# A one-core attention and two-layer MoE kernel: one unit's logits moved, a one-block order rewritten, filler products recounted

## The chip, the cores and the metric

The kernel runs on one core of a Trainium2 chip. The metric is device time in microseconds (us) of one execution; lower is better. In the profile PE is TensorE's matmuls, PEld its weight loads, DVE is VectorE, ACT is ScalarE, POOL is GpSimd and SP is SyncE; a q behind an engine's name is its sequencer or its DMA issue.

## The reference

A linear-attention recurrence over 768 steps (2 batches, 8 heads of 48) gives x with 1536 tokens of 384 numbers. Two mixture-of-experts layers follow, each with 8 experts (384 to 1024 to 384). The first adds a bias per modality to the logits; the second has a capacity of 384 tokens per expert:

```python
logits = x @ w_gate + modality_bias[modality_id]     # layer 0
e_idx = np.argmax(logits, axis=1); gate_w = softmax(logits)[e_idx]
out[mask] = gate_w[mask, None] * (np.maximum(x[mask] @ w1[e], 0.0) @ w2[e])
# layer 1: the same on layer 0's output, without a bias, tokens past the capacity give 0
```

So layer 1's routing needs the logits of layer 0's output, for all tokens.

## The kernel before

Three parts run one after the other: attention (L186 to L602), MoE layer 0 and MoE layer 1, both by `moe()` (L954).

**Units.** A layer's tokens are gathered by expert into blocks of 128; up to two blocks of one expert are a unit. Six units (0 to 5) always run, up to 13 may. On these data layer 0 runs eight (0 to 7) and layer 1 ten. `body(j)` (L1277) reads the unit's kind from the routing and branches to `two(j)` (L1221, both blocks, weights stationary) or `one(j)` (L1165, block 1 alone, tokens stationary). In layer 0 units 6 and 7 are one-block units (branch at L1295, where `one` comes first), the rest two-block; in layer 1 units 1, 2, 7 and 8 are one-block (branch at L1300).

**Precision.** Every fp32 product is three products of high and low parts. The high parts of the next unit's weights are made by ACT (`hi`, L960), the low parts by DVE (`lo`, L963): ten pieces per unit, six of w1 (letters a to f, 512 wide) and four of w2 (g to j, 768 wide).

**The order is written by hand** (a manual schedule on all engines): each engine's queue is the program's order. In `one`, six stretches of side work stand between the main steps first(j,0), first(j,1), turn(j,0), turn(j,1), second(j,0), second(j,1); each takes one string of `ONE` (L75). Its letters: a to j a weight piece for the next unit (capital: the low part alone); 0 and 1 the relu of a half (`relu`, L1057: ACT at L1063, DVE at L1065); y and z the turn and the split of the previous unit's block 1 (`yturn3` L1137, `ysplit3` L1145); l its logits (`ylog3` L1149); x and X the turn of the next unit's block 0 or 1 (`xprep` L1015: three PE transposes, an ACT copy L1020, a DVE subtraction L1021); P and Q the gates (Q is a DVE reduce L1034 and a reciprocal L1035). `turn` (L1068) transposes the relu's result on PE (L1072), ACT copies it (hh, L1075), DVE subtracts (hl, L1076), and `second` (L1079, products at L1088) consumes both.

**Layer 1's logits in layer 0's tail.** `ylog3` computes a block's logits with nine bf16 products (L722), a DVE reduce (L723) and then the block's store (`store`, L1132, an indirect DMA issued by POOL). Units 0 to 4 do block 0's in the next unit; unit 5 does it within its own last products (`end`, L1270 to L1273), since it could be the last unit.

**The end of layer 0.** `rest(j)` (L1361) branches on the number of blocks (L1372): the next unit, or `last(j-1)` (L1324). `last` loads the logits of all stored tokens back from memory (lgd, SP, L1337), scales the last block (ACT L1343), transposes it (PE L1347), copies (ACT L1348), takes its logits (`logits`, PE L696), spreads them by a one-hot product (DVE L1350, PE L1351) and adds both (DVE L1354). `routing()` (L758) follows. Ahead of them in the program stand unit forms that this input doesn't take.

**Filler.** `warm()` (L752) runs products of ones while PE would wait: `WARM[i] * 512 / width` products, width from `WIDE` (L46). Indices 0 to 2 are in the routing, 3 and 4 ahead of a layer's first unit, around `xprep(0,1)` and before the transposes of L1317.

Of the kernel before, what the change touches and what calls it, by code (L numbers as in the profile page):

```python
# [9 lines left out]
F32 = mybir.dt.float32  # L10
# [18 lines left out]
P = 128  # L29
NC = N // P  # L30
KD = DM // P
KF = F // P
U = 2 * P
NU_MIN = N // U
# [8 lines left out]


WARM = (4, 12, 2, 15, 4)
WIDE = ((512, 512, 512, 512, 512), (512, 512, 128, 128, 128))  # L46
TP = (3, 4)
OHP = ((0, 6), (6, 10), (10, 12))
CEIL = 255.0 / 512.0
# [20 lines left out]
SCALE = 'ssv'  # L70
LATE = (1,)
ONE_FIRST = (6, 7)
RELU = "sv"
PB = (1, 3, 1, 2)
ONE = (('ecadfPyz', '01bQ', 'X', 'l', 'hgix', 'js'), ('badec0P', 'f1hQ', 'xX', 'i', 'j', 'g'))  # L75


class Ctx:
# [875 lines left out]
def moe(tc, c, m, route, run, layer, src, w1d, w2d, dst, wg2, wp2, zb, following, lgs=None, psum=None, bad=None, general=None, ykeep=None):  # L954
    nc = tc.nc
    n = f"_m{layer}{run}"
# [5 lines left out]
    def lo(p, eng):  # L962
        eng.tensor_sub(p[2], p[0], p[1].bitcast(F32))  # L963
# [12 lines left out]
    with ctx:  # L976
        ap = m.ap
        if psum is None:
            psum = ctx.enter_context(tc.tile_pool(name="mo_ps" + n, bufs=2, space=PSUM))
# [32 lines left out]
                hi(pc[i], nc.scalar)  # L1012
                lo(pc[i], nc.vector)

        def xprep(j, t):  # L1015
            ts = slice(t * P, t * P + P)
            pt = psum.tile([P, KD, P], F32, tag="tp", name=f"xp{j}{t}" + n, bufs=TP[layer])
            for kc in range(KD):
                nc.tensor.transpose(pt[:, kc], m.xg[j % 2][:, t, kc * P : (kc + 1) * P], c.ident)  # L1019
            nc.scalar.copy(m.xh[j % 2][:, :, ts], pt)  # L1020
            nc.vector.tensor_sub(m.xl[j % 2][:, :, ts], pt, m.xh[j % 2][:, :, ts].bitcast(F32))  # L1021
# [35 lines left out]
        def relu(j, half):  # L1057
            ph = st.pop(("p", j, half))
            h = ap.tile([P, 512], F32, tag=f"h{half}", name=f"h{j}{half}" + n, bufs=1)
            wd = 512 if half == 0 or j == 0 else 256  # L1060
            for a in range(0, 512, wd):
                if RELU[half] == "s" or wd == 512:
                    nc.scalar.activation(h[:, a : a + wd], ph[:, a : a + wd], AF.Relu)  # L1063
                else:
                    nc.vector.tensor_scalar(h[:, a : a + wd], ph[:, a : a + wd], 0.0, None, ALU.max)  # L1065
            st["h", j, half] = h
# [82 lines left out]
        def ylog3(j, t):  # L1149
            logits3(tc, psum, [m.yp], wp2, m.yo[j % 2][:, t : t + 1, DM:XW], f"_y{j}{t}" + n, "lg", 1)  # L1150
            store(j, t)
# [13 lines left out]
        def one(j, pc):  # L1165
            before = layer == 0 and j > 0
            plan = iter(ONE[layer])

            def work():
                for p in next(plan):  # L1170
                    if p == "x" or p == "X":
                        if j + 1 < NU:
                            xprep(j + 1, int(p == "X"))
                    elif p == "y":
                        if before:
                            if j < NU_MIN:
                                ylog3(j - 1, 0)
                            yturn3(j - 1, 1)
                    elif p == "z":
                        if before:  # L1180
                            ysplit3()
                    elif p == "l":
                        if before:
                            ylog3(j - 1, 1)
                    elif p == "P" or p == "Q":
                        gates(j, 1 + (p == "Q"))
                    elif p == "s":
                        if layer == 0 and j < NU_MIN - 1:
                            scale(j, 1, "s")
                    elif p == "0" or p == "1":  # L1190
                        relu(j, int(p))
                    else:
                        i = "abcdefghij".index(p.lower())
                        if pc:
                            if p.islower():
                                hi(pc[i], nc.scalar)
                            lo(pc[i], nc.vector)

            first(j, 0)
            own(j, 0)  # L1200
            work()
            first(j, 1)
            own(j, 1)
            work()
            turn(j, 0)
            work()
            turn(j, 1)
            own(j, 2)
            work()
            second(j, 0)  # L1210
            work()
            second(j, 1)
            work()
# [7 lines left out]
        def two(j, pc):  # L1221
            before = layer == 0 and j > 0
            first2(j, 0)
            if before:
                if j < NU_MIN:
                    ylog3(j - 1, 0)
                yturn3(j - 1, 1)
                ysplit3()
            gates(j, 1)
            own(j, 0)  # L1230
            if j or layer:
                split(pc, 0, 2)
            first2(j, 1)
            gates(j, 2)
            own(j, 1)
            if j or layer:
                split(pc, 2, 6)
            else:
                split(pc, 0, 3)
            second2(j, 0, 0)  # L1240
            if before:
                ylog3(j - 1, 1)
            first2(j, 2)
            own(j, 2)
            if j or layer:
                split(pc, 6, 9)
            else:
                split(pc, 3, 6)
            second2(j, 0, 1)
            first2(j, 3)  # L1250
            if j == layer == 0:
                split(pc, 6, 8)
            else:
                split(pc, 9, 10)
            second2(j, 1, 0)
            second2(j, 2, 0)
            if j + 1 < NU:
                for t in range(2):
                    xprep(j + 1, t)
            second2(j, 3, 0)  # L1260
            scale(j, 0, SCALE[1])
            if j == layer == 0:
                split(pc, 8, 10)

            def turned():
                yturn3(j, 0)
                ysplit3()


            end = layer == 0 and j >= NU_MIN - 1  # L1270
            second2(j, 1, 1, (turned, 4) if end else None)
            second2(j, 2, 1, (turned, 2) if layer == 0 and not end else None)
            second2(j, 3, 1, (lambda: ylog3(j, 0), 4) if end else None)  # L1273
            if layer == 0 and not end:
                scale(j, 1, "s")

        def body(j):  # L1277
# [46 lines left out]
        def last(j):  # L1324
            if layer:
                finish(j)
            else:

                sp = ap.tile([P, 512], F32, tag="h0", name=f"sp{j}" + n, bufs=1)
                ohp, ohc = sp[:, 0:P], sp[:, P : P + NC]  # L1330
                put = sp[:, P + NC : P + NC * (E + 1)].rearrange("p (c e) -> p c e", e=E)
                col = slice(2 * j + 1, 2 * j + 2)
                nc.vector.tensor_scalar(ohp, c.i1[:, :, 0], R.tp[:, col], None, ALU.is_equal)
                nc.vector.tensor_scalar(ohc, c.jx[:, 0:NC], R.tc[:, col], None, ALU.is_equal)

                pl = psum.tile([P, NC, E], F32, tag="tp", name=f"lq{j}" + n, bufs=TP[0])
                nc.sync.dma_start(lgs[0], dst.rearrange("(p j) e -> p j e", j=NC)[:, :, DM:XW])  # L1337
                er = EXPERT0[j % 2]
                m.raw.load(j % 2, *following, slice(er, er + 1), parts=(1,))

                for kc in range(KD):
                    ks = slice(kc * P, kc * P + P)
                    nc.scalar.activation(m.yo[j % 2][:, 1, ks], ykeep[1][:, ks], AF.Identity, scale=R.gate[:, col])  # L1343
                xT = ap.tile([P, KD, P], F32, tag="lxT", name=f"lx{j}" + n, bufs=1)
                for kc in range(KD):
                    pt = psum.tile([P, P], F32, tag="h" if kc == 1 else "tp", name=f"yt{j}{kc}" + n, bufs=2 if kc == 1 else TP[0])
                    nc.tensor.transpose(pt, m.yo[j % 2][:, 1, kc * P : (kc + 1) * P], c.ident)  # L1347
                    nc.scalar.copy(xT[:, kc], pt)  # L1348
                py = logits(tc, psum, [xT[:, kc] for kc in range(KD)], wg2, None, None, f"_y{j}1" + n, "lg", 1)
                nc.vector.tensor_tensor(put, py.unsqueeze(1).to_broadcast((P, NC, E)), ohc.unsqueeze(2).to_broadcast((P, NC, E)), ALU.mult)  # L1350
                nc.tensor.matmul(pl, lhsT=ohp, rhs=put, start=True, stop=True)  # L1351
                nc.vector.tensor_copy(m.yo[j % 2][:, 1, DM:XW], py)
                store(j, 1)
                nc.vector.tensor_add(lgs[1], lgs[0], pl)  # L1354

                if j % 2 == 0:
                    for p in p0:
                        hi(p, nc.scalar)
                        lo(p, nc.vector)
# [142 lines left out]
```

## Time and profile before

| | us |
|---|---|
| median of 3 runs | 452.92 (452.83 to 454.48) |
| profiled execution, its own time | 451.07 |
| its span | 449.3 |
| mean granted TensorE clock | 0.979 of full speed |

Busy shares of the span: PE 93%, PEld 85%, DVE 73%, ACT 55%, POOL 32%. By the timeline, unit 5 of layer 0 runs from 220.9 to about 241, unit 6 to 252.3, unit 7 to 264.9; `last(7)` runs from 267.2 to 273.5, layer 1's routing to 282.6, and layer 1's first real products start at 287.5. A line of a timeline gives start and duration in us, engine, source line, operation, output<-inputs, shapes, a count, and in brackets the engine's idle time before it with what ended it.

### The profile page before, as it was taken

How to read it: one execution, taken by the hardware profiler on the slowest of the kernel's cores; microseconds unless marked ns; L12 is line 12 of the kernel's file. 1: busy time of each engine (PE TensorE's matmuls, PEld its weight loads, DVE VectorE, ACT ScalarE, POOL GpSimd, SP SyncE). 2: the span in 40 equal slices, each digit the busy share in tenths (PEclk: the TensorE clock that was granted, in tenths of full speed). 3: DMA queues.
4: the chain of work that ended last, by engine and by line, in shares of the span. 5: the costliest groups of instructions: out<-in, count | busy, mean ns of one | idle time of the engine just before them, and what ended most of it. 6: DMA issues, size and time to landing. Idle time of an engine off the chain costs nothing. (4 is left out here: it accounts for less than half of the span.)

```text
span 449.3 us, 9663 instructions
## 1 busy us (share of the span) xinstructions
PE 417.9 (93%) x3270; PEld 380.1 (85%) x3275; DVE 329.5 (73%) x677; ACT 249.3 (55%) x508; POOL 143.3 (32%) x160
## 2 busy tenths in 40 slices
PE   8999999999899999999999956999999999999990
PEld 4789988987389999999997854899899999998990
DVE  7798867984879859677597975386974945859760
ACT  3256545543537647557475840277864755777650
POOL 5637963141230422213223300503343132124420
PEclk9999999999899999999999996999999999999996
DMA  6987237348630121366744945314887657761100
GB/s 113 200 148 152 48 56 194 74 169 324 197 91 2 56 79 54 109 205 222 256 147 134 292 129 154 91 20 131 319 281 258 228 187 232 237 230 52 50 22 20
DMA packets 85590, 66.98 MB, mean 149 GB/s; under 512 B 60586, under 2 KB 77655, under 8 KB 85504
## 3 DMA queue, kind: packets, MB, share of 16 engines
q1 hardware_dynamic: 80512, 52.30, 39.8%
q0 software_dynamic: 4992, 13.61, 9.9%
q8 instruction: 44, 0.72, 0.7%
q14 instruction: 42, 0.34, 0.2%
HBM read 95.63 MB, written 11.56 MB: 239 GB/s over the span
## 5 line engine op out<-in xcount | busy, mean ns | idle before, releaser
L963 DVE TENSOR_TENSOR w1l<-w1r,w1h 128x512 fp32r<-128x512 f32 x114 | 71.7, 686 | 9.6 <-ACT w1h L960 9.4
L963 DVE TENSOR_TENSOR w2l<-w2r,w2h 128x768 fp32r<-128x768 f32 x76 | 69.2, 951 | 0.3 <-ACT w2h L960 0.3
L960 ACT CAST w1h<-w1r 128x512 fp32r<-128x512 f32 x114 | 62.7, 617 | 0.3 <-DMA xs<-zv 0.3
L1107 DVE SCALAR_TENSOR_TENSOR qhl_m<-qh_m,qhh_m 128x512 fp32r<-128x512 f32 x48 | 33.0, 686 | 36.0 <-ACT qhh_m L1106 36.0
L960 ACT CAST w2h<-w2r 128x768 fp32r<-128x768 f32 x76 | 59.4, 835 | 0.0
L1106 ACT ACTIVATE qhh_m<-qh_m 128x512 fp32r<-128x512 f32 x48 | 28.8, 599 | 41.7 <-PE qh_m L1101 41.7
L1101 PE MATMUL qh_m<-xh,w1h 128*128 128x256 f32 x288 | 51.0, 286 | 0.3 <-ACT xh L1318 0.2
L1101 PE MATMUL qh_m<-xl,w1h 128*128 128x256 f32 x288 | 50.2, 283 | 0.6 <-DVE w2l L963 0.6
L1119 PE MATMUL y_m<-w2h,qhh_m 128*128 128x384 f32 x192 | 50.0, 341 | 0.0
L1101 PE MATMUL qh_m<-xh,w1l 128*128 128x256 f32 x288 | 49.8, 282 | 0.0
L1119 PE MATMUL y_m<-w2l,qhh_m 128*128 128x384 f32 x192 | 49.6, 339 | 0.0
L1119 PE MATMUL y_m<-w2h,qhl_m 128*128 128x384 f32 x192 | 49.3, 338 | 0.0
L1004 POOL DMA_INDIRECT xg<-x,idg_l x24 | 26.0, 1083 | 69.2 <-DVE gd L1029 43.3
L1004 POOL DMA_INDIRECT xg<-xs,idg_l x20 | 22.2, 1111 | 67.2 <-issue 54.7
L1101 PEld LDWEIGHTS qh_m<-xh,w1h 128*128 128x128 f32 x288 | 42.6, 188 | 0.8 <-ACT xh L1318 0.8
L1101 PEld LDWEIGHTS qh_m<-xl,w1h 128*128 128x128 f32 x288 | 40.9, 188 | 1.2 <-DVE w2l L963 1.0
L1101 PEld LDWEIGHTS qh_m<-xh,w1l 128*128 128x128 f32 x288 | 40.9, 188 | 0.0
L1132 POOL DMA_INDIRECT out_dram<-yo,ids_l x20 | 22.1, 1103 | 49.3 <-ACT w2h L960 11.5
L1127 ACT ACTIVATE yo<-y_m,gate_l 128x384 f32<-128x384 f32 x29 | 16.9, 582 | 36.6 <-PE y_m L1119 28.9
L1020 ACT CAST xh<-xp_m 128x384 fp32r<-128x384 f32 x38 | 16.7, 485 | 35.8 <-PE xp_m L1019 35.8
L397 ACT ACTIVATE X<-endt,Sb 112x112 f32<-112x112 f32 x40 | 14.2, 354 | 38.5 <-PE endt L387 27.2
L1132 POOL DMA_INDIRECT x<-yo,ids_l x14 | 17.5, 1251 | 54.4 <-DVE qhl_m L1107 23.9
(252 smaller groups left out, 892.9 us busy)
## 6 DMA issues: line engine op xcount, KB each, us to landing
w2r<-in_moe_w_dram SPq DMA_DIRECT2D x50, 768.0 KB
w1r<-in_moe_w_dram SPq DMA_DIRECT2D x72, 512.0 KB
xs<-zv SPq DMA_DIRECT2D x12, 192.0 KB
out_dram<-zt SPq DMA_DIRECT2D x4, 576.0 KB
raw_w<-in_w_dram SPq DMA_DIRECT2D x14, 144.0 KB
raw_r<-in_r_dram SPq DMA_DIRECT2D x14, 144.0 KB
raw_k<-in_k_dram SPq DMA_DIRECT2D x14, 144.0 KB
raw_v<-in_v_dram SPq DMA_DIRECT2D x14, 144.0 KB
```

Source lines behind the costliest of these rows:

```text
L397: nc.scalar.activation(Xn, z, AF.Identity, scale=Tn)
L960: (eng.copy if eng is nc.scalar else eng.tensor_copy)(p[1], p[0])
L963: eng.tensor_sub(p[2], p[0], p[1].bitcast(F32))
L1004: nc.gpsimd.indirect_dma_start(out=m.xg[j % 2][:, t], out_offset=None, in_=src, in_offset=bass.IndirectOffsetOnAxis(ap=R.idg[:, 2 * j + t ...
L1020: nc.scalar.copy(m.xh[j % 2][:, :, ts], pt)
L1101: nc.tensor.matmul(ph[:, f], lhsT=w[s][:, kc, fs], rhs=a[s][:, kc], start=(i == 0), stop=(i == 3 * KD - 1))
L1106: nc.scalar.activation(hh, ph, AF.Relu)
L1107: nc.vector.scalar_tensor_tensor(hl, ph, 0.0, hh.bitcast(F32), ALU.max, ALU.subtract)
L1119: nc.tensor.matmul(st["y", j, t], lhsT=a[:, f, ts], rhs=w[s][:, 2 * q + f], start=(q == 0 and i == 0), stop=(q == 3 and i == 5))
L1127: nc.scalar.activation(m.yo[j % 2][:, t, 0:DM], py, AF.Identity, scale=R.gate[:, 2 * j + t : 2 * j + t + 1])
L1132: nc.gpsimd.indirect_dma_start(out=dst, out_offset=bass.IndirectOffsetOnAxis(ap=R.ids[:, 2 * j + t : 2 * j + t + 1], axis=0), in_=m.yo[j % ...
```

## The change

Five edits:

- `WIDE`: layer 1's filler 2 and 3 (8 and 60 products of 128 columns) become 2 and 15 products of 512 columns.
- `RELU`: in layer 0's one-block form the second half's relu goes from DVE to ACT, still as two pieces of 256.
- `ONE[0]`: z moves behind the relu of half 0, Q from the second stretch to the fifth, x from the fifth to the fourth (ahead of second(j,0)).
- x in layer 0's one-block form takes a PSUM buffer of tag "h" in place of "tp".
- Block 0's logits and store of unit 5 leave unit 5's tail: they are in unit 6, or in `last(5)` where there is no unit 6. Unit 5's `yturn3`/`ysplit3` of block 0 moves from within second2(5,1,1) to within second2(5,2,1).

```diff
-WIDE = ((512, 512, 512, 512, 512), (512, 512, 128, 128, 128))
+WIDE = ((512, 512, 512, 512, 512), (512, 512, 512, 512, 128))
-RELU = "sv"
+RELU = ("ss", "sv")
-ONE = (('ecadfPyz', '01bQ', 'X', 'l', 'hgix', 'js'), ('badec0P', 'f1hQ', 'xX', 'i', 'j', 'g'))
+ONE = (('ecadfPy', '01zb', 'X', 'lx', 'Qhgi', 'js'), ('badec0P', 'f1hQ', 'xX', 'i', 'j', 'g'))
-        def xprep(j, t):
+        def xprep(j, t, tag="tp"):
-            pt = psum.tile([P, KD, P], F32, tag="tp", name=f"xp{j}{t}" + n, bufs=TP[layer])
+            pt = psum.tile([P, KD, P], F32, tag=tag, name=f"xp{j}{t}" + n, bufs=TP[layer] if tag == "tp" else 2)
-                if RELU[half] == "s" or wd == 512:
+                if RELU[layer][half] == "s" or wd == 512:
-                            xprep(j + 1, int(p == "X"))
+                            xprep(j + 1, int(p == "X"), "h" if p == "x" and layer == 0 else "tp")
...
-                            if j < NU_MIN:
+                            if j <= NU_MIN:
                                 ylog3(j - 1, 0)
...
-            end = layer == 0 and j >= NU_MIN - 1
+            end = layer == 0 and j >= NU_MIN
             second2(j, 1, 1, (turned, 4) if end else None)
             second2(j, 2, 1, (turned, 2) if layer == 0 and not end else None)
             second2(j, 3, 1, (lambda: ylog3(j, 0), 4) if end else None)
-            if layer == 0 and not end:
+            if layer == 0 and j < NU_MIN - 1:
                 scale(j, 1, "s")
...
+                if j < NU_MIN:
+                    ylog3(j, 0)
                 pl = psum.tile([P, NC, E], F32, tag="tp", name=f"lq{j}" + n, bufs=TP[0])
```

The `j <= NU_MIN` line stands in `one` and in `two`; the last two lines added are in `last`.

## Rows read from the trace of the kernel before

**Rows 1.** Stretches: length; PE, PEld, DVE, ACT, POOL busy (count); clock, DMA share, GB/s
```profile
241.30:252.30 11.00, 10.96 (x78) 10.21 (x79) 10.42 (x22) 9.08 (x17) 4.36 (x4) 1.00 0.88 268
252.30:265.00 12.70, 11.04 (x78) 9.87 (x77) 12.15 (x26) 9.56 (x18) 3.75 (x3) 1.00 0.75 250
265.00:273.30 8.30, 2.65 (x11) 2.22 (x11) 2.01 (x7) 1.52 (x6) 0.00 (x0) 0.79 0.40 86
273.30:287.50 14.20, 11.66 (x120) 8.16 (x122) 8.53 (x37) 0.83 (x4) 5.06 (x5) 0.88 0.39 126
```

**Rows 2.** Timeline, the end of unit 5 and the start of unit 6
```profile
239.66 0.52 PE L722 MATMUL l_y_m<-wp,yp 128*128 128x24 bf16 x9
...
241.34 0.48 PE L1053 MATMUL ph_m<-w1h,xh 128*128 128x512 f32 x1 [0.72 <-ACT yo L1127]
...
241.84 0.69 DVE L963 TENSOR_TENSOR w1l<-w1r,w1h 128x512 fp32r<-128x512 f32 x1 [0.48 <-ACT w1h L960]
```

**Rows 3.** Timeline of DVE, PE and ACT, the middle of unit 7
```profile
258.85 0.75 DVE L1065 TENSOR_SCALAR h_m<-ph_m 128x256 f32<-128x256 f32 x2
...
259.32 0.77 PE L1072 MATMUL hp_m<-ident,h_m 128*128 128x128 f32 x4 [1.56 <-DVE h_m L1065]
...
259.52 0.68 DVE L963 TENSOR_TENSOR w1l<-w1r,w1h 128x512 fp32r<-128x512 f32 x1
...
260.12 0.17 DVE L1034 TENSOR_REDUCE gm<-gd 128x2 f32<-128x18 f32 x1
...
260.13 0.59 ACT L1075 CAST hh_m<-hp_m 128x512 fp32r<-128x512 f32 x1 [1.69 <-PE hp_m L1072]
...
260.40 0.67 DVE L1076 TENSOR_TENSOR hl_m<-hp_m,hh_m 128x512 fp32r<-128x512 f32 x1
...
261.45 0.68 DVE L1076 TENSOR_TENSOR hl_m<-hp_m,hh_m 128x512 fp32r<-128x512 f32 x1
...
262.05 0.17 DVE L723 TENSOR_REDUCE yo<-l_y_m 128x8 f32<-128x24 f32 x1
```

**Rows 4.** Groups by line and form: busy us, mean ns of one, idle before
```profile
L1020 ACT CAST xh<-xp_m 128x384 fp32r<-128x384 f32 x38 | 16.7, 485 | 35.8 <-PE xp_m L1019 35.8
...
L1065 DVE TENSOR_SCALAR h_m<-ph_m 128x256 f32<-128x256 f32 x12 | 4.5, 416 | 0.0
L1063 ACT ACTIVATE h_m<-ph_m 128x512 f32<-128x512 f32 x6 | 3.6, 599 | 0.1
```

**Rows 5.** Line 1372, 262 to 270 us: durations min/median/max in ns, first and last start
```profile
L1372 PEldq COMPARE_BRANCH  x1: 4701/4701/4701, 262.9 to 262.9; - x1
```

**Rows 6.** Timeline from unit 7's end to the last logits of layer 0
```profile
263.00 1.02 POOL L1132 DMA_INDIRECT x<-yo,ids_l  x1 [5.24 <-ACT w2h L960]
...
267.69 0.60 SPq L1337 DMA_DIRECT2D lgd<-x  x1
...
270.92 1.24 PE L696 MATMUL lpl_y_m<-wg,lx_m 128*128 128x8 f32 x6 [2.49 <-issue]
...
273.28 0.26 DVE L1354 TENSOR_TENSOR lg<-lgd,lq_m 128x96 f32<-128x96 f32 x1 [0.76 <-PE lq_m L1351]
```

**Rows 7.** Line 1132, 262 to 275 us: POOL's waits, and its transfers' landing
```profile
L1132 POOLq EVENT_SEMAPHORE  x4: 17/834/5985, 256.3 to 270.9; - x4
...
DMA to landing us min/median/max: 4.7/4.8/4.9
```

**Rows 8.** DMA view, 17.5 to 82 us: instruction packets, MB, share
```profile
q8 instruction: 6, 0.10, 0.6%
```

**Rows 9.** Stretch of straight code in the attention, columns as in rows 1
```profile
17.50:82.00 64.50, 62.84 (x639) 55.47 (x639) 51.62 (x82) 34.34 (x92) 38.26 (x50) 1.00 0.65 130
```

**Rows 10.** Timeline, PE ahead of layer 1's first unit
```profile
281.34 3.51 PE L755 MATMUL warm_m<-i,ones 128*128 128x128 bf16 x60
...
286.78 0.55 PE L1317 MATMUL xp_m<-ident,xg 128*128 128x128 f32 x3 [0.70 <-DMA xg<-x,idg_l]
```

**Rows 11.** Line 1300, layer 1, 288 to 440 us: PE's branches into a unit's form
```profile
L1300 PEldq COMPARE_BRANCH  x15: 65/191/419, 302.2 to 434.3; - x15
```

More of the change, by code (lines that the diff above doesn't have):

```diff
@@ L1224, in two @@
             if before:
-                if j < NU_MIN:
+                if j <= NU_MIN:
                     ylog3(j - 1, 0)
```

## The prediction

> **What bounds the kernel now.** The page first: PE is busy 93% of the span, so over the kernel as a whole only TensorE counts, and an edit that takes work from DVE or ACT should be worth nothing. The stretches view corrects this for the place where nearly all of the change lies [rows 1]. In units 6 and 7 DVE is busy 10.42 of 11.00 and 12.15 of 12.70 us: there DVE is the full engine. PE waits for it: before unit 7's second turn it sits idle 1.56 us until DVE's relu is done [rows 3]. In the next stretch, `last(7)`, nobody is busy: PE works 2.65 of 8.30 us. That stretch is pure waiting, and the timeline shows on what. PE's branch at L1372, out of unit 7 over the forms not taken, lasts 4.70 us [rows 5]; after it, PE stops once more for 2.49 us between two products of one group (L696), and the releaser given is "issue": it waited for no data [rows 6].
>
> That branch starts at 262.9. The last thing that PE's queue waits for ahead of it is hl of unit 7's second half, DVE's subtraction at 261.45 + 0.68 = 262.13 [rows 3]. So the tail of layer 0 is timed by DVE's chain through units 6 and 7, then by a jump, then by that stop. All my sums are for the end of L1354, which begins at 273.28 [rows 6]; the routing follows it directly.
>
> **Unit 5's tail.** The logits of block 0 sit in PE's queue ahead of the last two products, and they wait for DVE's split. PE then reads unit 6's branch after that wait, and sits idle 0.72 us before unit 6's first product; DVE's first low part follows at 241.84 after 0.48 us of waiting for ACT's high part [rows 2]. Without the logits' wait, the branch is read while earlier products still run. PE gains up to 0.37 us (the logits' slot, 239.66 to 240.03 by the count of products that follow) and most of the 0.72. DVE, which matters, gains between 0 (if ACT's high part stays the last to come) and about 0.8; I take 0.5, since ACT's own scale waits for PE's last product and so moves with PE. The nine products move into unit 6, where PE has slack: nothing, under the cover of DVE's chain. DVE's reduce moves there too: such a one takes 0.17 us, of which 0.08 overlap the instruction ahead (262.13 against 262.05) [rows 3]; it costs 0.09. What is queued behind the logits in unit 6 is the turn y, which no engine needs for a microsecond; POOL's store of block 0 goes later too, with the gathers behind it in POOL's queue for a unit that lies two ahead.
>
> **The relu moved to ACT.** Two pieces per unit leave DVE; they take 259.52 - 258.85 = 0.67 us of its queue [rows 3], two units: **1.34**. ACT gets them. No row has 256 columns on ACT: 384 take 485 ns and 512 take 599 [rows 4], so by that line about 0.37 each, an estimate, 0.74 per unit. ACT is busy 9.08 of 11.00 and 9.56 of 12.70 us [rows 1], and idle 1.69 us just before the copy of the second turn [rows 3], so I cost it at nothing, covered by that idle time. If the cover is gone (hi b and the first turn's copy stand behind the relus in ACT's queue, and DVE's low part of b stands behind hi b), it costs up to 0.74 per unit. I take 0.15 per unit, near the covered end because the idle time is over twice the work: **-0.3** in all.
> The Trainium skill, in "ScalarE: Activation LUTs", section "Rules for kernel authors", says to do relu on VectorE and not on ScalarE. By that rule the relus would have stayed and the sum below would be 1.34 us poorer. It is a rule for one instruction; here 256 columns take DVE 416 ns on average [rows 4], and which engine is full decides.
>
> **The order.** Q (reduce and reciprocal) stands on DVE right ahead of the first turn's subtraction: 260.40 - 260.12 = **0.28** us [rows 3] that leave the chain in unit 7; in unit 6 they only move later in the same chain. z moves behind the relu of half 0, which is ACT's work: the split of yp then comes later, and the logits (l) that need it stand two stretches on, so nothing. x goes ahead of second(j,0): its three transposes delay that product on PE, which waits there for DVE anyway; its DVE subtraction comes before the low parts h, g, i, after the last hl, so outside the chain. The "h" bank that it takes is one that both relus have read by then: free.
>
> **The chain so far:** 0.5 - 0.09 + 1.34 + 0.28 - 0.3 = **1.73 us** earlier at hl, and so at PE's branch; the 4.70 of the jump moves along unchanged.
>
> **The stop at L696.** In straight code the trace has 6 instruction packets [rows 8] over 639 products and 639 loads [rows 9], so one per some 213 of the recorded PE instructions if they were all PE's. The stop comes seven products and loads or so past the jump's target, with nothing to wait for: I read it as a new piece of code that had not arrived. Then where it falls depends on how many instructions stand ahead of it in the program. The change adds nine products and nine loads to `one(6)` and to `two(6)`, takes them out of `two(5)`, (what it adds to `last(5)` lies behind): 18 net ahead of `last(7)`, more if a copy of these forms stands there. The piece's edge then falls 18 or more instructions earlier, ahead of the target, and what lies behind it comes with the jump's own fetch. Anywhere at random, it would hit the 22 recorded instructions of this stretch [rows 1] 22 times in 213, one in ten. Without the stop PE would allow L1354 2.49 us earlier. What is late next is lgd: logits of unit 6's block, reduced at 262.05, stored by POOL at 263.00 [rows 6], landed 4.7 us later [rows 7], loaded by SP at 267.69 [rows 6], read by 270.9, when POOL's last wait before the next store begins [rows 7]. That chain moves with DVE too, so lgd allows the end 273.28 - 270.9 = 2.38 us earlier beyond the shift. I take **2.3**; the bounds are 0 (the stop stays) and 2.49.
> The Trainium skill, in "Runtime: NRT & Kernel Launch", section "Instruction fetch mechanics", has code refilled in blocks, crossing an edge mostly hidden, and a fetch to wait for where a taken branch leaves the window. The 4.70 agrees with the last. By its "mostly hidden" the 2.49 would be something else and stay: that is the first rival.
>
> **Filler and clock.** 60 narrow products take 3.51 us [rows 10], and 15 wide ones have the same columns; what follows waits 0.70 us for the gathered block anyway [rows 10], so 0, bounds 0 and +0.3. The clock is granted at 0.79 and 0.88 over the two stretches after unit 7 [rows 1], that is at half (1.2 of 2.4 GHz) for part of each, after PE stood idle. The change shortens the idle time and does not remove it: 0.
>
> **The sum:** 1.73 + 2.3 = 4.0 us off the profiled 451.07, so 447.0; that execution lies 1.85 under the median of 452.92, so against the runs **448.9**. About 0.5% (2.3 us) is what a measurement of this kernel can tell from no change.
>
> **Rivals.**
> 1. *The stop stays* or falls elsewhere inside `last(7)` (it isn't code, or the edge lands there again): 1.73 remain, 451.2. For: the rule above. Against: no engine has anything to deliver at 270.9. Chance 0.19.
> 2. *ACT binds units 6 and 7*: its 0.74 per unit is on the path, and 1.34 is not gained but 0.14 lost beyond it: chain 0.5 - 0.09 + 0.28 - 0.14 = 0.55, with the stop gone 2.85, 450.1; with it, 452.4. For: DVE's idle time at unit 6's start is for ACT [rows 2]. Against: 1.9 and 3.1 us of ACT idle [rows 1]. Chance 0.13.
> 3. *Slower: a piece's edge moves to a jump of layer 1.* Its units branch at L1300 and now pay 0.42 at most [rows 11]; a jump whose target isn't there pays up to 4.7, as L1372 does. It decides when a target lies just past the fetched code. One such jump gives 448.9 + 4.3 = 453.2, two give 457.5; with rival 1 one is enough for 455.5. For: all later code shifts too. Against: none of 15 pays it now. Slower by over 0.5%: 0.06.
>
> **How the numbers follow.** My forecast has 0.6, the rivals 0.19, 0.13 and 0.08 (0.06 of it slower, 0.02 within the bound). Faster by over 0.5%: 0.6, 0.04 of rival 1 (its gain is just under the bound) and 0.08 of rival 2 (stop gone), **0.72**. Within: 0.15 + 0.05 + 0.02, **0.22**. Slower: **0.06**. The range: low end 447.4, from ACT's 0.3 not lost, unit 5 giving 0.8, 0.3 of filler and some 0.6 of scatter between runs; high end 451.7, rival 1 with 0.5 of ACT's loss.
>
> **What would show it.** Right: unit 6 starts near 240.8; no PE idle of 1.56 before L1072; PE's branch at L1372 at about 261.1, still 4.7 long; no "issue" idle inside L696; DVE at L1354 near 269.3, after lgd and not after PE; layer 1's first products near 283.5. Wrong in the stop: over 2 us of "issue" at L696 or L1347. Wrong in the relu: DVE idle behind ACT at L960 or L1075 in units 6 and 7 by over half a us more. Wrong altogether: PE branches over 2 us at L1300.

## The result, and the profile after

| | before | changed | ratio, 95% interval |
|---|---|---|---|
| first measurement, 6 runs each, median | 453.31 | 449.38 | 0.9908 (0.9882 to 0.9935) |
| once more, on another chip, 19 and 8 runs | 451.01 | 448.93 | 0.9939 (0.9915 to 0.9963) |
| profiled execution | 451.07 | 449.44 | |

The change gains 2 to 4 us, 0.6 to 0.9%. The kernel before has medians from 450.5 to 453.6 on the chips used here, so below only ratios of runs on one chip are compared, and traces by their stretches. The ratios are as recorded for the runs; they are not the quotients of the two medians (0.9913 and 0.9954 here). The traces differ by 1.6 us in span: the execution shown ahead of the prediction lay below the other runs of its kernel on the first chip.

The timeline of the changed kernel, from unit 5's end to layer 1's first product (start, duration, then as before; line numbers from L1336 on are 2 higher):

```profile
239.37 0.39 PE L1053 MATMUL ph_m<-w1h,xh 128*128 128x512 f32 x1
...
240.93 3.10 DVE L963 TENSOR_TENSOR w1l<-w1r,w1h 128x512 fp32r<-128x512 f32 x5 [0.40 <-ACT w1h L960]
...
256.68 0.63 PE L1072 MATMUL hp_m<-ident,h_m 128*128 128x128 f32 x4 [0.75 <-DVE yr_m L1143]
...
259.11 0.68 DVE L1076 TENSOR_TENSOR hl_m<-hp_m,hh_m 128x512 fp32r<-128x512 f32 x1
...
266.54 0.61 SPq L1339 DMA_DIRECT2D lgd<-x  x1
...
267.48 0.87 PE L1349 MATMUL yt_m<-ident,yo 128*128 128x128 f32 x3 [5.12 <-issue]
...
268.29 1.45 PE L696 MATMUL lpl_y_m<-wg,lx_m 128*128 128x8 f32 x6
...
270.86 0.26 DVE L1356 TENSOR_TENSOR lg<-lgd,lq_m 128x96 f32<-128x96 f32 x1 [0.76 <-PE lq_m L1353]
...
285.44 0.73 PE L1101 MATMUL qh_m<-xh,w1h 128*128 128x256 f32 x3 [0.73 <-ACT xh L1318]
```

Against [rows 2, 3, 6]: unit 6 starts 1.97 us earlier on PE and 0.91 on DVE. The last hl ends at 259.79, 2.34 us earlier than 262.13. The six products at L696 run without a stop; the logits are added at 270.86, 2.42 us earlier. Layer 1 starts at 285.44; before, this line was at 287.53.

Part of this lies ahead of all that the edits alter in what runs: unit 5's first product starts 0.42 us earlier too, and up to it both kernels run the same work. Its line in the kernel before and in the changed one:

```profile
220.89 0.52 PE L1101 MATMUL qh_m<-xh,w1h 128*128 128x256 f32 x3
```

```profile
220.47 0.52 PE L1101 MATMUL qh_m<-xh,w1h 128*128 128x256 f32 x3
```

Counted from that product, unit 6 starts 1.55 us earlier on PE and 0.49 on DVE, the last hl ends 1.92 earlier, the logits are added 2.0 earlier, and the end comes 1.2 earlier. In a second pair of traces (e5 and e11 below) the last hl again gains 1.9, the logits' adding 2.6 and the end 2.9.

So DVE delivers 1.9 us earlier and a stop of 2.49 us is gone, and yet the end of layer 0 gains 2.0, about one of the two. The branches of PE's sequencer show where the other went. The line view of L1295 (out of unit 7's form) in the kernel before, a row not shown yet:

```profile
L1295 PEldq COMPARE_BRANCH  x1: 632/632/632, 262.2 to 262.2; - x1
```

and L1295 and L1374 (L1372 before) in the changed kernel:

```profile
L1295 PEldq COMPARE_BRANCH  x1: 2765/2765/2765, 259.8 to 259.8; - x1
...
L1374 PEldq COMPARE_BRANCH  x1: 4647/4647/4647, 262.7 to 262.7; - x1
```

PE comes to the exit of unit 7 2.4 us earlier (1.9 counted from unit 5), but the exit takes 2.77 us in place of 0.63. The long jump then begins 0.2 us earlier than in [rows 5], and 0.2 later counted from unit 5. DVE's whole gain is handed over to a new wait, and the time saved is the old stop's.

### The profile page after: what moved, and what is told of

It reads as the page before. It is cut to its first block, busy times and chain, and to the rows that moved or that the text cites. A ratio compares the mean times of both kernels' runs of the same rounds, so it can differ in the third digit from the quotient of the medians.

```text
span 447.7 us, 9559 instructions
## 1 busy us (share of the span) xinstructions
PE 418.6 (94%) x3219; PEld 378.5 (85%) x3224; DVE 327.9 (73%) x673; ACT 249.1 (56%) x512; POOL 144.2 (32%) x160
## 5 line engine op out<-in xcount | busy, mean ns | idle before, releaser
L1101 PE MATMUL qh_m<-xh,w1h 128*128 128x256 f32 x288 | 51.1, 286 | 0.9 <-ACT xh L1318 0.7
L1101 PE MATMUL qh_m<-xl,w1h 128*128 128x256 f32 x288 | 50.1, 282 | 0.7 <-DVE w2l L963 0.7
L1101 PE MATMUL qh_m<-xh,w1l 128*128 128x256 f32 x288 | 49.8, 281 | 0.0
L1101 PEld LDWEIGHTS qh_m<-xh,w1h 128*128 128x128 f32 x288 | 42.5, 188 | 1.3 <-ACT xh L1318 1.3
L1101 PEld LDWEIGHTS qh_m<-xl,w1h 128*128 128x128 f32 x288 | 40.9, 188 | 1.1 <-DVE w2l L963 1.1
L1101 PEld LDWEIGHTS qh_m<-xh,w1l 128*128 128x128 f32 x288 | 40.9, 188 | 0.0
L1119 PEld LDWEIGHTS y_m<-w2h,qhl_m 128*128 128x128 f32 x192 | 34.8, 188 | 0.0
```

The costliest lines, as they stand in the source:

```text
L1101: nc.tensor.matmul(ph[:, f], lhsT=w[s][:, kc, fs], rhs=a[s][:, kc], start=(i == 0), stop=(i == 3 * KD - 1))
L1119: nc.tensor.matmul(st["y", j, t], lhsT=a[:, f, ts], rhs=w[s][:, 2 * q + f], start=(q == 0 and i == 0), stop=(q == 3 and i == 5))
```

## The experiments

Twelve runs; the kernels of a group ran on one chip (e1 to e4; e5 to e8; e9 to e11, and e12 later on the same chip). "Never-run products" stand in a unit form that these data do not take: they move the code behind them and nothing else. In these kernels a line of the program has a number up to 13 higher.

| run | median | before on that chip | ratio (interval) | PE's exit from unit 7, us |
|---|---|---|---|---|
| e1 relu alone | 453.40 | 453.61 | 0.9997 (0.9976 to 1.0018) | 3.11 |
| e2 changed, logits stay | 454.70 | 453.61 | 1.0014 (0.9987 to 1.0041) | 3.41 |
| e3 before, 9 never-run | 450.89 | 453.61 | 0.9919 (0.9896 to 0.9943) | 0.55 |
| e4 changed, 32 and 96 never-run | 452.20 | 453.61 | 0.9942 (0.9911 to 0.9973) | 0.29 |
| e6 changed, narrow filler | 448.14 | 451.17 | 0.9929 (0.9905 to 0.9954) | 3.17 |
| e8 changed, edge put back | 454.05 | 451.17 | 1.0046 (1.0014 to 1.0078) | 3.29 |
| e9 logits stay, places kept | 450.23 | 451.01 | 0.9988 (0.9974 to 1.0002) | 3.55 |
| e10 unit 7's loads moved | 446.98 | 451.01 | 0.9907 (0.9880 to 0.9934) | 1.45 |
| e11 changed again | 448.93 | 451.01 | 0.9939 (0.9915 to 0.9963) | 2.79 |
| e12 changed, relu on DVE | 447.09 | 450.52 | 0.9925 (0.9906 to 0.9944) | 0.39 |

e5 (before again: 451.33, exit 0.55) and e7 (no loads: 446.30, exit 1.53) had one execution each.

### Is the stop at L696 code that has not arrived?

**e3**, nine products added to the kernel before where they never run:

```diff
+PAD = {5: 9}
             second(j, 1)
             work()
+            pad(j)      # layer 0's one(5): PAD[j] products of ones into a PSUM buffer
```

> The kernel before with nine products added in a form of unit 5 that is never taken (the one-block form): nothing that runs changes, only the code behind it lies 18 instructions further on. Theory 2 (the 2.49 us at L696 are a piece of code that has not arrived): the stop goes, L1354 ends 2 to 2.4 us earlier after the jump, and the run is about 2 us shorter, unless a new wait for code appears at another jump (then that wait shows in a branch row at L1295 or L1300). Rival (the stop is anything else): 2.4 to 2.5 us at L696 as before and the same time.

Timeline of PE, from unit 5's first product to layer 1's, and the branch out of unit 7 (L1304 here):

```profile
219.62 0.52 PE L1102 MATMUL qh_m<-xh,w1h 128*128 128x256 f32 x3
...
267.64 1.45 PE L697 MATMUL lpl_y_m<-wg,lx_m 128*128 128x8 f32 x6
...
281.85 0.33 PE L756 MATMUL warm_m<-i,ones 128*128 128x128 bf16 x3 [0.47 <-issue]
282.61 0.33 PE L756 MATMUL warm_m<-i,ones 128*128 128x128 bf16 x3 [0.43 <-issue]
284.08 0.44 PE L756 MATMUL warm_m<-i,ones 128*128 128x128 bf16 x5 [1.14 <-issue]
...
287.47 0.90 PE L1102 MATMUL qh_m<-xh,w1h 128*128 128x256 f32 x3
```

```profile
L1304 PEldq COMPARE_BRANCH  x1: 550/550/550, 260.9 to 260.9; - x1
```

The stop is gone, and the run is 2.7 us shorter by the medians, about what the change is worth. The expectation of a new wait elsewhere came true too, though not at a branch: 2.0 us of "issue" in three stops among the 60 narrow filler products. So the trace does not show where the 2.7 us are. Counted from unit 5's first product, the logits are added at 50.6 us (52.4 before, 53.1 in e5), but layer 1 starts at 67.9 (66.6 before, 67.7 in e5): what was gained at the stop is lost again by then, most of it in the filler. The kernel before was not profiled on this chip, where its median is 453.61, so what its runs wait for there, and what of that nine products take away, stays open.

**e8** does the reverse on the changed kernel: 88 never-run products ahead of layer 0's end put an edge back, 40 behind it give layer 1 its places again.

```diff
+PAD = {8: 88}       # in one(8), not run; 40 more in last(5), not run
```

> The changed kernel with never-run products placed so that the edge of a piece falls again some ten instructions past the target of layer 0's last jump, and layer 1's code has the same place within its pieces as in the changed kernel (176 and 80 instructions added, 256 in all). Theory 2: the stop of 2.3 to 2.5 us at L696 is back, L1356's place comes 2.3 us later than in the changed kernel, and the run is about 2 us longer (451 to 452). Rival: no stop, time as the changed kernel, 449.4.

```profile
274.59 1.42 PE L697 MATMUL lpl_y_m<-wg,lx_m 128*128 128x8 f32 x6 [5.53 <-issue]
```

The stop is back at the same place, at 5.53 us more than twice as long as expected, and the kernel is slower than before the change. **e5**, the kernel before once more, has it at its old size:

> The kernel before, unchanged, for a second profile: the profiled execution shown ahead of the prediction (451.07) lies under the runs of the same kernel (453.6 on average). If waits for code differ from one execution to the next, this profile shows another sum of long branches and 'issue' stops than the first (0.63 at L1295, 4.70 at L1372, 2.49 at L696) by about as much as its span differs. If they are the same to 0.2 us and the span differs by over 1 us, the scatter lies elsewhere (attention, DMA).

```profile
270.56 1.24 PE L696 MATMUL lpl_y_m<-wg,lx_m 128*128 128x8 f32 x6 [2.50 <-issue]
```

Its exit took 0.55 and its long branch 4.87: the first profile's waits within 0.2 us, in a run of 451.33. Both profiles of the kernel before are of executions of about 451 us; one of 453 was not profiled, and what such a one waits for stays open. The stop's place is the place of the code: one run without it, one with it, and nothing else that runs changed. A packet of code ends each of these stops. DMA view, instruction packets of 16 KB, of the kernel before from 268 to 270 us, and of e8 from 272 to 274.59 (e8 has none from 268.03, the end of its long jump, to 272):

```profile
q8 instruction: 1, 0.02, 4.3%
```

```profile
q8 instruction: 1, 0.02, 2.1%
```

PE goes on 1.3, 1.4 and 1.7 us after the packet has landed (before, e5, e8). How long the stop lasts (2.49, 2.50, 5.53) goes with the packet, which starts 0.7 us after the long jump's end in the first two and 4.0 in e8; why it is that late in e8 was not tried.

### What DVE's chain gained, and from which edit

I measure the chain from DVE's first low part of unit 6 to the end of unit 7's last hl: 241.84 to 262.13 is 20.29 us before (and in e5), 240.93 to 259.79 is 18.86 in the changed kernel.

**e1**, the relu alone:

```diff
-RELU = "sv"
+RELU = ("ss", "sv")
-                if RELU[half] == "s" or wd == 512:
+                if RELU[layer][half] == "s" or wd == 512:
```

> The kernel before with one edit: the second half's relu of layer 0's one-block form goes to ACT. Theory 1 (DVE's chain times units 6 and 7): hl of unit 7's second half ends 1.3 us earlier than in the kernel before (near 260.8), PE's wait ahead of its turn falls from 1.56 to under 0.7, and no engine pays for it. Rival (ACT binds): hl ends no earlier, and DVE waits for ACT in these units over 1 us more. The stop at L696 stays at 2.4 to 2.5 us if it is not code; if it is code, it may go, because PE's own wait instructions change with this edit. Time: 1.3 less than before if the stop stays, up to 3.7 less if it goes.

Timeline of ACT and DVE in unit 6, and the branch:

```profile
245.79 0.66 ACT L1063 ACTIVATE h_m<-ph_m 128x256 f32<-128x256 f32 x2 [1.10 <-PE ph_m L1053]
...
246.99 0.69 DVE L963 TENSOR_TENSOR w1l<-w1r,w1h 128x512 fp32r<-128x512 f32 x1 [0.94 <-ACT w1h L960]
```

```profile
L1295 PEldq COMPARE_BRANCH  x1: 3114/3114/3114, 261.5 to 261.5; - x1
```

The chain is 20.02 us: 0.27 gained of the 1.3 expected. ACT stands idle 1.10 us ahead of the moved relu, since PE has not finished the products that it reads; behind it in ACT's queue stands hi b, and DVE idles 0.94 us for that. The stop at L696 was gone here too. The edit is not free of a shift of the code: with the relu on ACT PE's queue has one instruction more in each of units 6 and 7, a wait ahead of the second turn. In unit 7:

```profile
L1072 PEldq EVENT_SEMAPHORE  x1: 51/51/51, 258.0 to 258.0; - x1
```

So 2.8 us less (0.27 and 2.49) would have been possible; but PE's exit took 3.11 us, 2.5 more than before, and among the narrow filler products the stops of e3 came again, the longest 1.15 us. Time unchanged.

**e2**, the logits of unit 5 back in unit 5:

```diff
-            end = layer == 0 and j >= NU_MIN
+            end = layer == 0 and j >= NU_MIN - 1
...
-                            if j <= NU_MIN:
+                            if j < NU_MIN:
                                 ylog3(j - 1, 0)
```

> The changed kernel with one edit undone: unit 5's logits of block 0 are back in unit 5's tail. Theory 1: unit 6 starts on DVE as in the kernel before (0.9 us later than in the changed kernel, first low part near 241.8) and that start is carried through to hl of unit 7, which ends 0.5 to 0.9 us later than in the changed kernel (near 260.5). Rival: the earlier start is lost again by unit 7, so hl ends where the changed kernel has it, 259.8. For code: the nine products are not moved past unit 6, so the long branch out of unit 7 at L1295 (2.77 us in the changed kernel, 0.63 before) should be near 0.6 if the place of the code sets it, and stay over 2 if it is the load on the DMA queues.

The chain is 19.84 (240.50 to 260.34). The exit was not near 0.6 but 3.41, so the nine products' place did not set it. And it lost the change's whole gain, mostly not where the logits are. Line view of layer 1's branches:

```profile
L1300 PEldq COMPARE_BRANCH  x15: 65/286/3283, 301.4 to 437.3; - x15
```

Against 0.42 at most in [rows 11]: three of them took 3.06, 2.43 and 3.28 us, and PE, when its earlier products had run out, stood idle 0.7, 0.2 and 2.7 us. Undoing the edit moved layer 1's code too. **e9** is the same kernel with never-run products that put units 7 and later, layer 0's end and layer 1 back where the changed kernel has them:

```diff
+PAD = {5: 9, 8: 18}    # and 10 products in last(5), not run
```

> The changed kernel with unit 5's logits back in unit 5's tail, as in the run that undid this before, but with never-run products (9 ahead of unit 6, 18 ahead of layer 0's end, 10 behind it) that put units 7 and later, layer 0's end and layer 1 at the places in the code that the changed kernel has. Theory 2: the three branches of 2.4 to 3.3 us at L1300 that the undoing brought are gone (under 0.5 each), so most of its loss was the place of the code; what is left against the changed kernel is the move's own worth, 0 to 0.9 us (unit 6 starting later). About 449.5 to 450.5 where the changed kernel has 449.4 and the kernel before 453.3; in the same ratio on another chip (0.992 to 0.994). Rival (the move of the logits itself saves 4 us): as slow as the kernel before, ratio 0.998 to 1.003.

```profile
246.14 0.69 DVE L964 TENSOR_TENSOR w1l<-w1r,w1h 128x512 fp32r<-128x512 f32 x1 [1.17 <-ACT w1h L961]
```

```profile
L1309 PEldq COMPARE_BRANCH  x15: 65/188/423, 301.4 to 433.5; - x15
```

The branches of layer 1 are short again, and more than half of e2's loss is gone: from unit 5's first product to the end it takes 229.0 us, against 232.9 in e2 and 227.2 and 226.8 in the two profiles of the changed kernel. What is left by the runs, 0.9988 against 0.9939 for the changed kernel on the same chip, is more than the 0 to 0.9 us that I gave the move, though less than the rival's 4 us. The trace says why: the chain is 19.93 us, so with relu and order but without the logits' move 0.36 us are gained, with it 1.43. With unit 6's earlier start on PE, ACT waits for PE 0.69 us ahead of the relu in place of 1.10 in e1, and DVE's low part behind it does not wait at all. Unit 6 of the changed kernel:

```profile
244.40 0.66 ACT L1063 ACTIVATE h_m<-ph_m 128x256 f32<-128x256 f32 x2 [0.69 <-PE ph_m L1053]
...
245.60 0.69 DVE L963 TENSOR_TENSOR w1l<-w1r,w1h 128x512 fp32r<-128x512 f32 x1
```

Against e11 below, and counted from unit 5, e9 adds the logits 2.7 us later: 1.6 of them are DVE's start and chain, 1.2 PE's exit and the long jump behind it.

**e11** is the changed kernel itself, on that chip:

> The changed kernel, unchanged, beside the others on one chip and for a second profile. Expected: ratio to the kernel before 0.990 to 0.994 as first measured; L1295 between 2.5 and 3.4 us again and no stop at L696.

Its exit took 2.79 us and there was no stop at L696; its chain is 18.85 us.

**e12** checks the relu from the other side, back on DVE with the rest of the change kept:

```diff
-RELU = ("ss", "sv")
+RELU = ("sv", "sv")
+PAD = {5: 3, 8: 8}
```

> The changed kernel with the second half's relu back on DVE, and 11 never-run products that keep units 7 and later, layer 0's end and layer 1 at the places in the code that the changed kernel has. Theory 4 (the relu's move pays only together with the logits' move: alone, ACT stood waiting for PE ahead of it in unit 6 and DVE idled 0.94 to 1.17 us for hi b; with unit 6 starting 2 us earlier on PE it doesn't): without it hl of unit 7 ends 0.9 to 1.4 us later than in the changed kernel, DVE has no idle time over 0.5 us in units 6 and 7, PE waits again for DVE's relu ahead of unit 7's second turn. Of this little or nothing reaches the end, because PE's exit waits for code until 262.4 anyway: L1295 falls by about as much as hl comes later, and the run is 0 to 1 us longer than the changed kernel (ratio to before 0.993 to 0.997 on this chip's scale, where the changed kernel had 0.994). Rival: the relu's 1.3 us are lost in full at the end, ratio 0.997 or more.

```profile
256.35 0.77 PE L1073 MATMUL hp_m<-ident,h_m 128*128 128x128 f32 x4 [1.07 <-DVE h_m L1066]
...
269.04 0.25 DVE L1365 TENSOR_TENSOR lg<-lgd,lq_m 128x96 f32<-128x96 f32 x1 [0.94 <-DMA lgd<-x]
```

```profile
L1304 PEldq COMPARE_BRANCH  x1: 391/391/391, 259.8 to 259.8; - x1
```

The chain is 19.80 (239.95 to 259.75), 0.94 longer than with the relu on ACT, as expected. But the run is not longer. Its exit takes 0.39 in place of 2.8, the logits are added at 269.04 against 271.24 in e11, and the span is 445.1 against 447.5. Of both differences 1.26 us are there already at unit 5's first product (219.49 and 220.75), so 0.9 and 1.1 are this edit's. By medians 447.09 against 448.93; the intervals of the two ratios overlap, so that it is faster rests on the traces, one of e12 and two of the changed kernel. Moving the relu shortened DVE's work and lengthened PE's exit by more.

### Why the exit from unit 7 is long

**e7** leaves out the weight loads that units 6 and 7 issue (layer 1's first units then compute with what the buffers hold):

```diff
-            loads(j + 2)
+            if not (layer == 0 and run == "" and j in (6, 7)):
+                loads(j + 2)
```

> The changed kernel without the weight loads that units 6 and 7 of layer 0 issue (layer 1's first two units then compute with weights left in the buffers). Code and its place on PE are the same. Theory 3 (the piece of code that PE needs at its exit from unit 7 waits behind weights in the DMA queues): the branch at L1295 falls from 2.77 to under 1 us, and the next branch starts at 260.0 to 260.5. Rival (the fetch is only asked for at the branch): still over 1.5 us, about 0.7 to the packet, 1 us of packet and 1.3 to the resumption, less little for an idle queue.

**e10** leaves no load out and moves one, unit 7's w1, into `last(7)`:

```diff
+            if layer == 0 and run == "" and j == 8:
+                loads(j + 1)
-            loads(j + 2)
+            if not (layer == 0 and run == "" and j == 7):
+                loads(j + 2)
...
-                m.raw.load(j % 2, *following, slice(er, er + 1), parts=(1,))
+                m.raw.load(j % 2, *following, slice(er, er + 1), parts=(0, 1) if j == 7 and run == "" else (1,))
```

> The changed kernel with the w1 load that unit 7 issues for layer 1's second unit moved into layer 0's end (SP, behind the load of the logits), where the DMA queues are idle. PE's code is the same. Theory 3 (the piece that PE's exit from unit 7 needs waits in full DMA queues): L1295 falls from 2.8 to between 1.3 and 2.0 us (1.53 without any loads in units 6 and 7), layer 1 starts 0.8 to 1.4 us earlier, the run is about 1 us shorter than the changed kernel. Rival: the fetch is not delayed by these weights, L1295 stays over 2.5 and the time is that of the changed kernel; or the later load is late for layer 1, which would show as waits for w1r in its first unit.

Stretches ahead of the exit, columns as in [rows 1], where the last two are the DMA share and GB/s: the changed kernel, then e7, then e10.

```profile
256.00:258.00 2.00, 1.19 (x17) 1.11 (x17) 1.93 (x5) 1.82 (x4) 1.50 (x2) 1.00 1.01 395
258.00:260.00 2.00, 2.00 (x14) 2.00 (x13) 2.00 (x6) 1.77 (x3) 0.00 (x0) 1.00 1.02 403
```

```profile
256.00:258.00 2.00, 1.49 (x18) 1.41 (x19) 1.93 (x5) 1.54 (x5) 0.04 (x1) 1.00 0.39 111
258.00:260.00 2.00, 2.00 (x14) 2.00 (x13) 2.00 (x6) 2.00 (x4) 0.00 (x0) 1.00 0.10 32
```

```profile
256.00:258.00 2.00, 1.05 (x15) 0.88 (x15) 1.93 (x5) 1.82 (x5) 1.69 (x2) 1.00 0.28 72
258.00:260.00 2.00, 2.00 (x16) 2.00 (x15) 2.00 (x5) 1.70 (x4) 0.03 (x1) 1.00 0.60 115
```

With the DMA engines full the exit takes 2.77, with them at 0.1 to 0.6 it takes 1.53 and 1.45: some 1.3 us are the piece of code waiting among weights. The packet of code starts 0.2 us after PE reaches the exit in the changed kernel, 0.8 and 0.9 us before that in e7 and e10. e7's 1.53 fell short of the "under 1" that was expected, so that is half of the story. The rest is when the piece comes. DMA view, instruction packets, of the changed kernel from 259.5 to 262 us (it has none from 253 to 259.5):

```profile
q8 instruction: 1, 0.02, 2.7%
```

and of e12 from 257 to 258.5 (none from 253 to 257):

```profile
q8 instruction: 1, 0.02, 4.0%
```

In e12 the DMA engines were as full from 256 to 258 (share 1.00), and the packet came 2.6 us sooner (257.43 against 260.08), with DVE's last hl at the same time (259.75 and 259.79). Counted from PE's second turn it came after 1.1 us, in the changed kernel after 3.4. Over all fourteen profiles the exit is 0.39 to 0.63 in the four with the relu on DVE (before, e5, e3, e12), 2.77 to 3.55 in the seven with it on ACT and all loads, and 1.53 and 1.45 in e7 and e10; only e4 stands apart. Why the fetch comes later when the relu ahead of PE's second turn is ACT's was not settled; the one wait more in PE's queue (e1) is one thing that differs, and it was not tried alone.

**e4** tried to have it asked for sooner, by moving the code so that an edge lies at the start of unit 7's form:

```diff
+PAD = {5: 32, 8: 96}
```

> The changed kernel with 32 products added in unit 5's form that is never taken and 96 in unit 8's, which is not run: 64 instructions ahead of units 6 and 7, 256 in all ahead of layer 0's end. Theory 2: with these 64 the edge of a piece comes at the very start of unit 7's one-block form and not in its middle, so the next piece is asked for some 5 us earlier and is there when PE leaves unit 7; the branch at L1295 falls from 2.77 to about 0.3 us, the branch at L1372's place starts 2.4 us earlier, and the end of layer 0 comes 1 to 2.4 us earlier, bounded then by the load of the logits (issued at 266.5 in the changed kernel). The stop at L696 stays away. Rival (the branch waits for a queue full of weights): 2.5 us or more at L1295 as in the changed kernel, same time.

```profile
255.37 0.39 PE L1054 MATMUL ph_m<-w1h,xl 128*128 128x512 f32 x1 [3.65 <-DVE w1l L964]
255.37 0.19 PEld L1054 LDWEIGHTS ph_m<-w1l,xh 128*128 128x128 f32 x1 [3.86 <-issue]
```

The exit fell to 0.29 as expected, and PE paid for it at the other end: after the first product of unit 7 it stopped for 3.86 us (the releaser named, DVE's low part, was not it: the weight load's line says "issue"), and the exit from unit 5 took 1.77. The expectation had named the edge's new place and not asked what it would cost there. Its span, 450.7, is 3.0 over the changed kernel's, but by the ratios (0.9942 and 0.9908, on two chips) the intervals overlap.

### The filler

**e6**, layer 1's filler back at 128 columns:

```diff
-WIDE = ((512, 512, 512, 512, 512), (512, 512, 512, 512, 128))
+WIDE = ((512, 512, 512, 512, 512), (512, 512, 128, 128, 128))
```

> The changed kernel with the filler of layer 1 back at 128 columns (51 products more, so 102 instructions more, inside the routing). Forecast of the prediction: 0 to 0.3 us longer. Theory 2 (place and amount of code): the edge of a piece now falls among the narrow filler products, where the run with nine never-run products had 1.14 us of 'issue' at L755 and slower products around it, and layer 1's units lie 102 instructions further on; so 1 to 3 us longer, to be seen as issue stops at L755 and long branches at L1300. Rival: filler is hidden behind the gather, same time.

```profile
279.61 3.51 PE L755 MATMUL warm_m<-i,ones 128*128 128x128 bf16 x60
```

```profile
L1300 PEldq COMPARE_BRANCH  x15: 65/181/2605, 299.5 to 432.2; - x15
```

No stop among the narrow products this time, two branches of 2.6 us in layer 1 (PE still had products to run meanwhile and stood idle only 0.2 and 0.3 us), a shorter jump out of it (3.65 against 4.75), and a ratio of 0.9929, between the two that the changed kernel has. No worth of the filler's width by itself shows; the 102 instructions less are a move of the code behind them, and which way that goes is particular to the program: in e1 and e3 the same filler held stops of 2.0 us.

## Why the prediction came out right, and where it was wrong

The time was right (449.4 against 448.9) and the range held it, but not by the sum that gave it. The sum took 4.0 us off layer 0's end, 1.73 from DVE's chain and 2.3 from the stop. Counted from unit 5, the two pairs of traces show 2.0 and 2.6 there: the chain gave 1.9, the stop 2.5, and PE's exit from unit 7, which the sum does not have, took 2.1 back. That the medians of the first chip lie 3.9 apart all the same, as forecast, is in part luck: on the second chip they lie 2.1 apart, and the two pairs of traces have 1.2 and 2.9 at the end. Of the signs that were to show the forecast right, three did not come: L1372's branch at about 261.1 (it came at 262.7), the adding near 269.3 behind lgd (270.86, behind PE) and layer 1 near 283.5 (285.44).

- **DVE's chain, 1.73 forecast: 1.92 measured** (2.34 with what lay ahead of unit 5). The sizes are near: DVE's start gained 0.49 where I had 0.5, the rest of the chain 1.43 where I had 1.23. The reason given for one of them fails. By e1, e2, e9 and e12 the relu alone gives 0.27, relu and order 0.36 to 0.45, and the relu 0.94 once the logits are moved. The step that failed is "I cost it at nothing, covered by that idle time": the idle time that I named stands in unit 7, and in unit 6 ACT itself waits for PE, 1.10 us, with hi b behind. It was the start of unit 6 on PE, 1.55 us earlier, that covered it. I had put that at up to 1.1 for PE and drawn nothing from it for ACT.
- **"The 4.70 of the jump moves along unchanged".** It did not: the jump's own length held (4.65), but ahead of it stands another, PE's exit from unit 7, which I had not priced: 0.63 became 2.77. So the step "and so at PE's branch" failed: counted from unit 5, that branch begins 0.2 us later than before, and the chain's whole gain is given back. It is a wait for code, as in the third rival, in a place that the rival did not name; and a moved edge alone does not explain it, since e12 has the code from unit 7 on at the same places and an exit of 0.39. In layer 1, which the rival named, the changed kernel has nothing over 0.42, while e2 shows how near that was.
- **The stop at L696, 2.3 forecast: gone.** The reading as code that had not arrived is shown by e3 and e8. What I took to be late next, the load of the logits, was not: PE waits for its jump until 267.48, then the adding waits for PE. In e10 and e12, where PE comes sooner, the adding does wait for lgd, 1.00 and 0.94 us.
- **The jump and the page.** The Trainium skill, "Runtime: NRT & Kernel Launch", section "Instruction fetch mechanics", calls the crossing of an edge mostly hidden. In straight code the trace agrees (PE busy 62.84 of 64.50 us over six packets [rows 8, 9]); just past a jump it does not, with 2.49 to 5.53 us at L696 and 3.86 in e4. The first rival, which I drew from it, falls.
- **The clock, forecast 0.** Stretches of the changed kernel from PE's exit to layer 1, columns as in [rows 1]:

```profile
262.40:270.90 8.50, 2.99 (x11) 2.36 (x11) 2.53 (x7) 1.57 (x6) 0.00 (x0) 0.74 0.43 95
270.90:285.40 14.50, 12.69 (x69) 6.12 (x70) 8.46 (x36) 0.75 (x3) 5.05 (x5) 0.80 0.40 127
```

  At 0.74 and 0.80 the lower level lasts longer than at the 0.79 and 0.88 of [rows 1]: twice the missing share, 10.2 us against 6.9. It fell mostly on filler: the 12 products of it in the routing took 4.45 us (3.34 before), and the routing's next product, L836, came 6.75 us after the logits' adding (6.52 before). Layer 1's products at L1101 take what they took before.
- **Q, z, x, filler.** Order and relu together are 0.36 us in e9; the order's own part was not run alone; in e12, with the logits moved and the relu on DVE, the chain is 0.49 shorter than before, where I had 0.19. For the filler no gain shows, as forecast.
- **The relu's place.** The Trainium skill, "ScalarE: Activation LUTs", section "Rules for kernel authors", would leave the relu on VectorE. e12 agrees in its result and not for the reason of speed: ACT's 256 columns take 382 ns and DVE's 416, DVE's chain is 0.94 us longer in e12, and the kernel is no slower, since PE's exit is 2.4 us shorter.

So of the 2.0 us that layer 0's end gains in the traces shown, the stop is all: the chain's 1.9 and the exit's 2.1 cancel. e8 agrees: with a stop back at that place, and a longer one, the changed kernel is slower than the kernel before. That an edit has worth of its own is shown for the logits' move alone, by e9 against e11 on one chip: half a per cent, with the code from unit 7 on at the same places.

## What to carry to other kernels

In a long program with branches, find out what an edit does to code behind it before its time is credited to the edit: shift the code with products that never run, before and after, and compare. Count two traces from a point ahead of what the edit alters, since executions differ there already. When one engine's chain is shortened, read the sequencer's branches next, since a jump that was in time can be the next to be late. And a load that is not needed soon belongs where no code is being fetched: moving one w1 load took 1.3 us off a jump.

## What was not expected of the hardware

An "issue" stop or a long branch of 2 to 5.5 us came and went with 18 to 256 instructions that never ran. A jump whose piece of code came in time took 0.3 us (e4, e12: 0.29, 0.39), one whose piece came late 2.4 to 3.6, the long jump out of layer 0's units 4.6 to 5.1 in every profile. The same exit took 1.2 to 1.3 us longer at a DMA share of 1.0 than at 0.1 to 0.6.

Two kernels look better than the changed one, by different edits: e10 (0.9907 against 0.9939 on one chip, span 445.7 against 447.5) and e12 (from unit 5 to the end 1.1 us shorter than e11). Their intervals overlap with the changed kernel's, and e10 and e12 were not run together.
